# Top-32 attention with a hardswish MLP on one core: later batches' keys and queries transposed by DMA, and duos 2 to 19 at the wider spacing

## The chip, the core and the metric

The kernel runs on one core of a Trainium2 chip. A core has TensorE (PE, with PEld for its weight loads), VectorE (DVE), ScalarE (ACT), GpSimd (POOL) and SyncE (SP, which here issues all DMAs). Each takes its own instructions strictly in order, and they wait for each other through semaphores. The metric is the device time of one execution in microseconds (us).

## The reference

Attention over 8 batches of 8 heads, 576 positions, head size 64. Of each row of scores only the 32 largest survive; the result goes through a two-layer MLP with hardswish.

```python
scores = scale * np.matmul(q, k.transpose(0, 1, 3, 2))
kth = np.partition(scores, -32, axis=-1)[..., -32:-32 + 1]
scores = np.where(scores >= kth, scores, -1e9)
scores = scores - np.max(scores, axis=-1, keepdims=True)
attn = np.exp(scores); attn = attn / (np.sum(attn, axis=-1, keepdims=True) + 1e-09)
x = np.matmul(attn, v)            # then (B,H,S,D) -> (B*S, H*D) = (4608, 512)
h = x @ w_in                      # (4608, 2048)
out = (h * np.clip(h + 3.0, 0.0, 6.0) / 6.0) @ w_out
```

q, k and v are float32. The two weights arrive as float64 and are turned into float32 on the chip.

## The kernel before

Two heads make a **pair** (64 + 64 rows of TensorE), four pairs a batch. A pair's keys and queries are loaded as they lie (`Pair.load`, one tile `landed` of 128 x 1152 floats), and `Pair.transpose` (L170 to L182) turns them with nine 128 x 128 TensorE transposes into the one PSUM buffer `big`, from which ACT copies them out into `kq` and `kr`. The same `big` takes the scores.

Two pairs and 128 query positions make a **duo**: two rows of 576 scores in each partition for each of its two pairs. There are 80 duos, counted here from 0, ten in a batch. The 576 positions are four times 128 and a rest of 64, so in each of the batches 0 to 6 the duos 2 and 7 of the batch (2, 7, 12, 17, ... 67) are **rest duos** with half the rows; in the last batch these are 72 and 73. The steps of a duo m are

- `scores`: TensorE into `big`, ACT copies to `sc` (L232, L235; L218, L219 for a rest). It is called in slot 1 of duo m-1.
- `top`: DVE, four rounds of MAX8 and three of MATCH_REPLACE8 for each pair (L249, L253). This is what a duo's eight **slots** are: slots 0 to 3 are the rounds of its first pair, 4 to 7 those of the second.
- `shift` (POOL, L262, L265), `exp` (ACT: two Prelu L272, two Exp L277, the sum's epsilon L282), `inverse` (DVE reciprocal, L286), `weights` (POOL: scale L296, then split of each float into two 16-bit halves into tile `e16`, L305), `flip` (SP: DMA transpose of `e16` into `t16`, L311), `join` (halves put together again into `eT`, by ACT for the first pair and by POOL for the second, L317), `values` (TensorE, L337, copied out by ACT, L344). A 0 or 1 behind a step's name is the pair.

When these steps are called is written out in three tables, in slots from the duo's own slot 0: `early` for duos 0 and 1, `soon` for 2 to 19 and the last two, `usual` for 20 to 77. Each engine gets its instructions in the order of the calls:

```python
usual = dict(shift0=3, exp0=4, inverse0=7, weights0=8, flip0=10, join0=13,
    shift1=7, exp1=8, inverse1=11, weights1=12, flip1=14, join1=17, values=20)
soon = dict(shift0=3, exp0=3, inverse0=5, weights0=5, flip0=7, join0=10,
    shift1=7, exp1=7, inverse1=9, weights1=9, flip1=11, join1=14, values=16)
```

Between them `piece` emits the MLP in small **pieces** (four or eight matmuls of the first layer, L361, or two of the second, L383), 3 to 9 to a duo by how many are left; ACT copies a first-layer result out twice (L369, L371) and POOL gates it (L375, L376). `values` of some duos first empties the block before the last (a loop of `piece()`), so a few places get many pieces at once. What is left at the end is done after the last duo. In the first four and a half duos the weights are converted as well (`convert`, L102 to L122, on all of SP, ACT, POOL and DVE).

The tiles `landed`, `kq`, `e16`, `t16`, `eT` and the weights' `st` share one pool of 13 buffers (tag `kq`). A new tile waits until the buffer's last reader is done. For batch b+1 the four pairs are loaded in slot 0 of duos 4 to 7 of batch b and transposed in slot 5 of duos 5 to 8.

Of the kernel before, what the change touches and what calls it, by code (L numbers as in the profile page):

```python
# [10 lines left out]
F32 = mybir.dt.float32  # L11
U32 = mybir.dt.uint32
I32 = mybir.dt.int32
U16 = mybir.dt.uint16
# [15 lines left out]
def kernel(  # L30
# [9 lines left out]
    nc = tc.nc  # L40
    P = nc.NUM_PARTITIONS
    B, H, S, D = q.shape
    DM, FF = moe_w_in.shape
    J = S // P
    JP = J * P
    R = S - JP
# [6 lines left out]
    def pool(name, bufs, **kw):  # L53
        return ctx.enter_context(tc.tile_pool(name=name, bufs=bufs, **kw))

    consts = pool("consts", 1)
    kqpool = pool("kq", 13)
# [30 lines left out]
    def big():  # L88

        return ps_big.tile([P, 5 * 512], F32, tag="big", name="big")  # L90
# [47 lines left out]
    class Pair:  # L138
# [31 lines left out]
        def transpose(self):  # L170
            kq = kqpool.tile([P, JP + S], F32, tag="kq", name="kq")
            self.kT, self.qT = kq[:, 0:JP], kq[:, JP : JP + S]
            ps = big()
            for j in range(2 * J + 1):
                rows = self.landed[:, j, :, :].rearrange("p h d -> p (h d)")
                nc.tensor.transpose(ps[:, j * P : (j + 1) * P], rows, ident[:])
            c0 = 2 * JP
            nc.scalar.copy(kq[:, 0:c0], ps[:, 0:c0])
            nc.scalar.copy(kq[:, c0 : c0 + R], ps[:, c0 + R : c0 + 2 * R])
            for hh in range(2):  # L180
                d = slice(hh * D, (hh + 1) * D)
                nc.scalar.copy(self.kr[d, hh, :], ps[d, c0 : c0 + R])  # L182

    class Duo:

# [122 lines left out]
        def flip(self, u):  # L308
            t16 = self.t16[u] = kqpool.tile([P, 2 * (2 * J + 1), P], U16, tag="kq", name="t16")
            n = 2 * self.nb  # L310
            nc.sync.dma_start_transpose(t16[:, 0:n, :], self.e16[u][:, 0 : n * P])  # L311

        def join(self, u):

            eT = self.eT[u] = kqpool.tile([P, 2 * J + 1, P], F32, tag="kq", name="eT")
            copy = nc.gpsimd.tensor_copy if u else nc.scalar.copy
            copy(  # L317
                eT[:, 0 : self.nb, :]
                .rearrange("p c q -> p (c q)")
                .bitcast(U16)  # L320
                .rearrange("p (x h) -> p h x", h=2),
                self.t16[u][:, 0 : 2 * self.nb, :].rearrange("p (h c) q -> p h (c q)", h=2),
            )
# [79 lines left out]
    for b in range(B):  # L403
        halves = [pairs[b][0:2], pairs[b][2:4]]
# [8 lines left out]
    per_batch = 2 * J + 2  # L413
    ND = len(duos)
# [5 lines left out]
    def piece(count=1):  # L420
        nonlocal left
        for _ in range(count):
            while todo:
                try:
                    gates.append(next(todo[0]))
                    left -= 1
                    break
                except StopIteration:
                    todo.pop(0)
            else:  # L430
                gates.append(None)
            if len(gates) > 2:
                gate = gates.pop(0)
                if gate:
                    gate()
# [54 lines left out]
    def convert_step(depth=2):  # L490

        if len(converting) >= depth or not landing:
            for c in converting[:1]:
                next(c, None)
            del converting[:1]
        if landing:
            c = landing.pop(0)
            next(c)
            converting.append(c)
        land()  # L500

    def pair_at(m, first):

        b, at = divmod(m, per_batch)
        return pairs[b + 1][at - first] if b + 1 < B and 0 <= at - first < NHP else None
# [18 lines left out]
    usual = dict(  # L524
        shift0=3, exp0=4, inverse0=7, weights0=8, flip0=10, join0=13,
        shift1=7, exp1=8, inverse1=11, weights1=12, flip1=14, join1=17, values=20,
    )
    early = dict(
        shift0=3, exp0=3, inverse0=4, weights0=4, flip0=5, join0=7,
        shift1=7, exp1=7, inverse1=8, weights1=8, flip1=9, join1=10, values=11,  # L530
    )
    soon = dict(
        shift0=3, exp0=3, inverse0=5, weights0=5, flip0=7, join0=10,
        shift1=7, exp1=7, inverse1=9, weights1=9, flip1=11, join1=14, values=16,
    )
    queued = {}
    for m in range(ND):
        for part, at in (early if m < 2 else soon if m < 2 * per_batch or m >= ND - 2 else usual).items():
            queued.setdefault(8 * m + at, []).append((m, part))

    def parts(slot):
        for m, part in sorted(queued.get(slot, []), key=lambda x: x[1][:-1] != "shift"):
            if part == "values":
                values(m)
            else:
                getattr(duos[m], part[:-1])(int(part[-1]))

    for m in range(ND + 3):
        u = duos[m] if m < ND else None

        level = (left >= 8) + (left >= 16) + (left >= 48)
        count = ((3, 4, 4, 5) if u and u.rest else (6, 7, 8, 9))[level]
        for i in range(8):
            if u:
                u.top(i // 4, i % 4)
            convert_step()
            if m == 0 and i == 0:
                first[3].load()
            if m == 0 and i in (1, 2):
                first[i + 1].transpose()  # L560
            if i == (3 if m == 0 else 1) and m + 1 < ND:
                duos[m + 1].scores()
            parts(8 * m + i)
            if m == 0 and i in (1, 4):
                for p in duos[i // 4].pairs:
                    p.load_values()
            if i == 0:
                p = pair_at(m, 4)
                if p:
                    p.load()  # L570
            if i == 3 and u and u.pairs[0].b and 1 <= m % per_batch <= 2:
                for p in duos[m - 1].pairs:
                    p.load_values()
            if i == 5:
                p = pair_at(m, 5)
                if p:
                    p.transpose()
            piece((i + 1) * count // 8 - i * count // 8)
    while todo:
        piece()  # L580
# [34 lines left out]
```

## Time and profile before

| what | us |
| --- | --- |
| median of 3 runs | 1680.22 (1679.17 to 1680.78) |
| the profiled execution | 1679.66 |
| its span (first to last instruction) | 1677.9 |
| busy PE / DVE / ACT / POOL in the span | 1481.3 / 1469.5 / 1089.3 / 1144.2 |

The profile is of one execution. Its span is cut into stretches at the starts of duos: DVE's first MAX8 comes at 13.6 us, duo 3 starts at 116.9, duo 20 at 478.6, duo 72 at 1434.8; DVE's last MAX8 ends at 1579.8, and from there to 1677.9 the rest of the MLP runs. An undisturbed full duo takes DVE 19.4 us, an undisturbed rest duo about 11. A row's idle time in brackets is that of the engine just before the instruction, with what ended it. TensorE's records of a float32 matmul come in two, so its counts are twice the program's.

### The profile page before, as it was taken

Reading aid. Unit: us, or ns where it says so; the run is one execution under the profiler, and the core shown is the slowest. Engines: PE = TensorE matmul, PEld = TensorE weight load, DVE = VectorE, ACT = ScalarE, POOL = GpSimd, SP = SyncE. Lnnn points to the kernel's source line nnn. Section 1 sums busy time; section 2 is a strip of 40 time slices with the busy share of each in tenths; the row PEclk is TensorE's granted clock in tenths of the full one; section 3 lists DMA queues with packets and bytes.
Section 4 is the critical chain, followed back from the end, with each engine's and each line's share of the span. In section 5 each row is a group of like instructions: output and inputs, shape, how many; then the busy total and the mean of one; then the engine's idle time right before and its main releaser. Section 6 shows DMA issues by size and latency. Waiting matters only on the chain.

```text
span 1677.9 us, 25630 instructions
## 1 busy us (share of the span) xinstructions
PE 1481.3 (88%) x8736; PEld 985.9 (59%) x8736; DVE 1469.5 (88%) x3105; ACT 1089.3 (65%) x1863; POOL 1144.2 (68%) x1266
## 2 busy tenths in 40 slices
PE   5245688756899999899999999898999999899999
PEld 2142456534646757575766666565676675656775
DVE  5899979899799989999999979999999979999600
ACT  5556656656657868686767857677767766766621
POOL 4887566655657868685857857786867866776741
PEclk9567789977899999999999999999999999999999
DMA  8462433434235363445344432545345423433410
GB/s 235 132 185 52 92 62 63 100 73 85 56 62 106 76 120 54 94 87 109 60 96 96 86 82 54 117 81 112 62 94 100 97 57 74 96 64 64 70 21 13
DMA packets 450307, 144.29 MB, mean 86 GB/s; under 512 B 433280, under 2 KB 441472, under 8 KB 450176
## 3 DMA queue, kind: packets, MB, share of 16 engines
q1 hardware_dynamic: 450176, 142.65, 40.5%
q8 instruction: 69, 1.13, 0.3%
q14 instruction: 62, 0.51, 0.1%
HBM read 45.09 MB, written 9.44 MB: 32 GB/s over the span
## 4 chain that ended last, share of the span: by engine, by line
PE 45%; DVE 31%; POOL 10%; ACT 6%; issue 5%; DMA 2%; SPq 1%; POOLq 0%; ACTq 0%
PE acc L383 17%; DVE m L249 16%; PE h L361 15%; DVE wk L253 13%; PE pv L337 6%; PE big L226 4%; POOL eT L317 3%; POOL e L305 3%; POOL sc L296 2%; ACT eT L317 2%; ACT sc L277 1%; PE big L229 1%; POOL g L376 1%; DVE y L118 1%; DMA t<-e 1%
## 5 line engine op out<-in xcount | busy, mean ns | idle before, releaser
L249 DVE MAX8 m<-wk 128x8 f32<-128x576 f32 x864 | 614.8, 749 | 2.9
L383 PE MATMUL acc<-w_out,g 128*128 128x512 f32 x1152 | 515.8, 598 | 7.0 <-POOL g L376 7.0
L361 PE MATMUL h<-xT,w_in 128*128 128x256 f32 (+1 forms) x2560 | 470.7, 342 | 2.0 <-ACT hs L371 2.0
L361 PEld LDWEIGHTS h<-xT,w_in 128*128 128x128 f32 x2560 | 407.6, 193 | 50.0 <-issue 9.1
L253 DVE MATCH_REPLACE8 wk<-m,wk 128x576 f32<-128x576 f32 x576 | 424.4, 744 | 0.0
L383 PEld LDWEIGHTS acc<-w_out,g 128*128 128x128 f32 x1152 | 213.3, 191 | 246.0 <-issue 235.8
L305 POOL COPY e<-sc 128x2304 uint16<-128x2304 uint16 (+1 forms) x192 | 323.8, 1696 | 10.1
L337 PE MATMUL pv<-eT,vm 128*64 128x128 f32 (+1 forms) x2560 | 177.3, 286 | 159.3 <-POOL eT L317 122.5
L296 POOL TENSOR_SCALAR sc<-sc,den 128x576 f32<-128x576 f32 x288 | 213.3, 750 | 138.8 <-DVE den L286 137.8
L337 PEld LDWEIGHTS pv<-eT,vm 128*64 128x64 f32 x2560 | 143.8, 148 | 206.1 <-POOL eT L317 129.2
L277 ACT ACTIVATE sc<-sc,shift 128x576 f32<-128x576 f32 x288 | 220.1, 767 | 65.4 <-POOL shift L265 62.8
L272 ACT ACTIVATE sc<-sc,m 128x576 f32<-128x576 f32 x288 | 209.7, 774 | 59.5 <-DVE m L249 59.2
L317 POOL COPY eT<-t 128x2304 uint16<-128x2304 uint16 (+1 forms) x80 | 208.3, 2604 | 10.4 <-DMA t<-e 10.3
L317 ACT COPY eT<-t 128x2304 uint16<-128x2304 uint16 (+1 forms) x80 | 209.3, 2616 | 4.5 <-DMA t<-e 4.5
L253 DVE MATCH_REPLACE8 wk<-m,sc 128x576 f32<-128x576 f32 x288 | 212.1, 744 | 0.0
L249 DVE MAX8 m<-sc 128x8 f32<-128x576 f32 x288 | 203.3, 744 | 1.0 <-ACT sc L235 1.0
L376 POOL TENSOR_TENSOR g<-g,hs 128x512 f32<-128x512 f32 x144 | 183.7, 1276 | 12.2 <-POOL g L375 0.2
L262 POOL TENSOR_TENSOR shift<-m 128x2 f32<-128x2 f32 (+1 forms) x160 | 32.7, 204 | 195.5 <-DVE den L286 186.8
L232 ACT COPY sc<-big 128x2048 f32<-128x2048 f32 (+1 forms) x65 | 119.5, 1838 | 59.8 <-PE big L229 59.3
L375 POOL TENSOR_SCALAR g<-g 128x512 f32<-128x512 f32 x144 | 88.5, 615 | 98.7 <-ACT g L369 88.8
L226 PE MATMUL big<-kq 64*128 64x512 f32 x512 | 143.8, 684 | 8.5 <-ACT kr L182 8.4
L344 ACT COPY xT<-pv 128x256 f32<-128x256 f32 x64 | 23.8, 372 | 185.8 <-PE pv L337 185.8
(47 smaller groups left out, 1193.6 us busy)
## 6 DMA issues: line engine op xcount, KB each, us to landing
landed<-in_k_dram SPq DMA_DIRECT2D x64, 128.0 KB, 2.8
landed<-in_q_dram SPq DMA_DIRECT2D x64, 128.0 KB, 2.9
st<-in_moe_w_in_dram SPq DMA_DIRECT2D x16, 512.0 KB, 5.3
vm<-in_v_dram SPq DMA_DIRECT2D x64, 128.0 KB, 2.3
st<-in_moe_w_out_dram SPq DMA_DIRECT2D x16, 512.0 KB, 4.6
out_dram<-o SPq DMA_DIRECT2D x32, 256.0 KB, 2.4
t<-e SPq DMA_TRANSPOSE x160, 4.6
landed<-in_k_dram SPq DMA_DIRECT2D x32, 32.0 KB, 2.5
```

The costliest lines, as they stand in the source:

```text
L226: nc.tensor.matmul(banks[:, 2 * i + hh, :], pr.qT[d, qs], pr.kT[d, :])
L249: nc.vector.max(self.m[u][:, t, 8 * r : 8 * r + 8], self.cur[t])
L253: nc.vector.match_replace(wk, self.m[u][:, t, 8 * r : 8 * r + 8], self.cur[t], LOWEST)
L272: nc.scalar.activation(row, row, AF.Prelu, bias=m[:, t, TOP_K - 1 : TOP_K], scale=-1.0, alpha=FLAT)
L277: nc.scalar.activation(row, row, AF.Exp, bias=self.less[u][:, t : t + 1], scale=-scale / FLAT, accum_out=self.den[:, u, t : t + 1],)
L296: nc.gpsimd.tensor_scalar(row, row, self.den[:, u, t : t + 1], 1.0, ALU.mult, ALU.mult)
L305: nc.gpsimd.tensor_copy(halves[:, :, to : to + c1 - c0], words)
L317: copy(eT[:, 0 : self.nb, :] .rearrange("p c q -> p (c q)") .bitcast(U16) .rearrange("p (x h) -> p h x", h=2), self.t16[u][:, 0 : 2 * self ...
L337: nc.tensor.matmul(pv[hh * D : (hh + 1) * D, u * w : (u + 1) * w], pr.vm[:, hh, c, :] if c < J else pr.vr[:, hh, :], rhs, start=(c == 0), ...
L361: nc.tensor.matmul(h[:, (f - f0) * nt : (f - f0 + 1) * nt], w_in[:, i, f * P : (f + 1) * P], xT[:, i, 0:nt], start=(i == 0), stop=(i == NH ...
L376: nc.gpsimd.tensor_tensor(g[:], g[:], hs[:], ALU.mult)
L383: nc.tensor.matmul(acc[:], gs[f // nf][:, c0 : c0 + P], w_out[:, f, :], start=(f == 0), stop=(f == NFC - 1),)
```

## The change

Three things change. The pairs of batches 1 to 7 are no longer transposed by TensorE: POOL splits `landed` into 16-bit halves (`split`), SP issues a DMA transpose (`flip`), and ACT puts the halves together in `kq` and `kr` (`join`, four copies). The load comes a duo earlier (slot 0 of duos 3 to 6 of a batch), split and flip stand in slots 2 and 5 of duos 4 to 7, the join in slot 1 of duos 5 to 8. And the table `soon` now holds for the last two duos alone, so duos 2 to 19 go by `usual`; in `early`, the flips, joins and values of duos 0 and 1 come one or two slots later. Batch 0 is transposed as before.

```diff
+        def split(self):
+            self.e16 = kqpool.tile([P, 2 * (2 * J + 1) * P], U16, tag="kq", name="e16")
+            nc.gpsimd.tensor_copy(
+                self.e16[:].rearrange("p (h x) -> p h x", h=2),
+                self.landed[:]
+                .rearrange("p j h d -> p (j h d)")
+                .bitcast(U16)
+                .rearrange("p (x h) -> p h x", h=2),
+            )
+
+        def flip(self):
+            self.t16 = kqpool.tile([P, 2 * (2 * J + 1), P], U16, tag="kq", name="t16")
+            nc.sync.dma_start_transpose(self.t16[:], self.e16[:])
+
+        def join(self):
+            kq = kqpool.tile([P, JP + S], F32, tag="kq", name="kq")
+            self.kT, self.qT = kq[:, 0:JP], kq[:, JP : JP + S]
+            halves = self.t16[:].rearrange("p (h c) q -> p h (c q)", h=2)
+
+            def copy(dst, src):
+                nc.scalar.copy(dst.bitcast(U16).rearrange("p (x h) -> p h x", h=2), src)
+
+            c0 = 2 * JP
+            copy(kq[:, 0:c0], halves[:, :, 0:c0])
+            copy(kq[:, c0 : c0 + R], halves[:, :, c0 + R : c0 + 2 * R])
+            for hh in range(2):
+                d = slice(hh * D, (hh + 1) * D)
+                copy(self.kr[d, hh, :], halves[d, :, c0 : c0 + R])
...
     early = dict(
-        shift0=3, exp0=3, inverse0=4, weights0=4, flip0=5, join0=7,
-        shift1=7, exp1=7, inverse1=8, weights1=8, flip1=9, join1=10, values=11,
+        shift0=3, exp0=3, inverse0=4, weights0=4, flip0=6, join0=8,
+        shift1=7, exp1=7, inverse1=8, weights1=8, flip1=10, join1=12, values=13,
     )
...
-        for part, at in (early if m < 2 else soon if m < 2 * per_batch or m >= ND - 2 else usual).items():
+        for part, at in (early if m < 2 else soon if m >= ND - 2 else usual).items():
...
             if i == 0:
-                p = pair_at(m, 4)
+                p = pair_at(m, 3)
                 if p:
                     p.load()
...
-            if i == 5:
-                p = pair_at(m, 5)
+            for at, first_at, part in ((2, 4, "split"), (5, 4, "flip"), (1, 5, "join")):
+                p = pair_at(m, first_at) if i == at else None
                 if p:
-                    p.transpose()
+                    getattr(p, part)()
```

DVE in rest duo 12, from the reciprocal of duo 11's second pair to that of duo 12's first pair; before:

```order
L286 RECIPROCAL den<-den 128x2
L249 MAX m<-wk 128x8
L253 MATCH_REPLACE wk<-m,wk 128x576
L249 MAX m<-wk 128x8
L249 MAX m<-sc 128x8
L253 MATCH_REPLACE wk<-m,sc 128x576
L249 MAX m<-wk 128x8
L253 MATCH_REPLACE wk<-m,wk 128x576
L286 RECIPROCAL den<-den 128x1
```

and now (the lines behind the new methods are 30 higher):

```order
L316 RECIPROCAL den<-den 128x2
L279 MAX m<-sc 128x8
L283 MATCH_REPLACE wk<-m,sc 128x576
L279 MAX m<-wk 128x8
L283 MATCH_REPLACE wk<-m,wk 128x576
L279 MAX m<-wk 128x8
L283 MATCH_REPLACE wk<-m,wk 128x576
L279 MAX m<-wk 128x8
L316 RECIPROCAL den<-den 128x1
```

The first reciprocal stood behind the second round of duo 12 and stands behind the fourth; the second stood behind the sixth and stands behind the eighth. (One row before the second piece is the fourth round's MAX.)

ACT in rest duo 37, from the copy of duo 38's scores; before:

```order
L232 COPY sc<-big 128x4x512
L235 COPY sc<-big 128x2x128
L369 ACTIVATE g<-h,three 128x512
L371 COPY hs<-h 128x512
L344 COPY xT<-pv 128x2x128
L272 ACTIVATE sc<-sc,m 128x576
L277 ACTIVATE sc,den<-sc,shift 128x576
L282 ACTIVATE den<-den 128x1
L317 COPY eT<-t_5686 128x2x1152
L178 COPY kq<-big 128x1024
```

and now:

```order
L262 COPY sc<-big 128x4x512
L265 COPY sc<-big 128x2x128
L205 COPY kq<-t_5542 128x2x1024
L205 COPY kq<-t_5542 128x2x64
L205 COPY kr_112<-t_5542 64x2x64 x2
L399 ACTIVATE g<-h,three 128x512
L401 COPY hs<-h 128x512
L374 COPY xT<-pv 128x2x128
L302 ACTIVATE sc<-sc,m 128x576
L307 ACTIVATE sc,den<-sc,shift 128x576
L312 ACTIVATE den<-den 128x1
L347 COPY eT<-t_5611 128x2x1152
```

The join of a pair of batch 4 (three rows, four copies, from a transposed tile `t`) now stands between the scores' copy and duo 37's exp; before, the copies from `big` stood behind that exp.

TensorE in duos 46 and 47, up to the scores of duo 48 (`kr_110`); before:

```order
L383 MATMUL acc<-w_out,g 128x512 x6
L337 MATMUL pv<-eT,vm_104 64x128 x8
L337 MATMUL pv<-eT,vr_108 64x128 x2
L337 MATMUL pv<-eT,vm_105 64x128 x8
L337 MATMUL pv<-eT,vr_109 64x128 x2
L383 MATMUL acc<-w_out,g 128x512 x2
L176 MATMUL big<-ident,landed 128x128 x9
L383 MATMUL acc<-w_out,g 128x512 x6
L226 MATMUL big<-kq 128x512 x4
L229 MATMUL big<-kr_110,kq 128x128
```

and now:

```order
L413 MATMUL acc<-w_out,g 128x512 x6
L367 MATMUL pv<-eT,vm_104 64x128 x8
L367 MATMUL pv<-eT,vr_108 64x128 x2
L367 MATMUL pv<-eT,vm_105 64x128 x8
L367 MATMUL pv<-eT,vr_109 64x128 x2
L413 MATMUL acc<-w_out,g 128x512 x8
L256 MATMUL big<-kq 128x512 x4
L259 MATMUL big<-kr_110,kq 128x128
```

The nine transposes between the pieces are gone; the pieces of the MLP and the values (`pv`) stand as they did.

## Rows read from the trace of the kernel before

**Rows 1.** Page, part 1: busy time, share of the span, instructions of each engine.

```profile
PE 1481.3 (88%) x8736; PEld 985.9 (59%) x8736; DVE 1469.5 (88%) x3105; ACT 1089.3 (65%) x1863; POOL 1144.2 (68%) x1266
```

**Rows 2.** DVE's waits to 116.9, to 478.6, to 1434.8: us, times, longest.

```profile
DVE den L286 <- ACT den L282: 15.4, 4, 7.5
...
DVE den L286 <- ACT den L282: 44.1, 19, 5.5
...
DVE den L286 <- ACT den L282: 27.0, 8, 10.0
```

**Rows 3.** Windows, stretches: length, busy PE, PEld, DVE, ACT, POOL, clock, DMA share, GB/s.

```profile
116.90:478.60 361.70, 269.13 (x1689) 181.48 (x1689) 316.57 (x669) 221.78 (x379) 230.41 (x255) 0.84 0.37 75
478.60:1434.80 956.20, 933.60 (x5378) 611.97 (x5373) 925.12 (x1986) 679.36 (x1165) 689.92 (x764) 0.99 0.43 87
...
1579.80:1677.90 98.10, 94.11 (x572) 67.34 (x570) 0.17 (x1) 22.27 (x38) 31.54 (x31) 0.99 0.13 23
```

**Rows 4.** Timeline, rest duo 12: start, length, engine, instruction, idle time before it.

```profile
318.33 0.78 ACT L277 ACTIVATE sc<-sc,shift 128x576 f32<-128x576 f32 x1 [4.06 <-POOL shift L265]
...
320.23 0.17 DVE L286 RECIPROCAL den<-den 128x2 f32<-128x2 f32 x1 [3.60 <-ACT den L282]
...
325.30 2.82 ACT L317 COPY eT<-t 128x2304 uint16<-128x2304 uint16 x1
...
329.97 0.16 DVE L286 RECIPROCAL den<-den 128x1 f32<-128x1 f32 x1 [4.10 <-ACT den L282]
```

**Rows 5.** Timeline, duo 0 into duo 1: ACT's join.

```profile
50.68 2.78 ACT L317 COPY eT<-t 128x2304 uint16<-128x2304 uint16 x1 [2.34 <-DMA t<-e]
```

**Rows 6.** Groups by line and form: count, busy us, mean ns, idle before.

```profile
L317 ACT COPY eT<-t 128x2304 uint16<-128x2304 uint16 x64 | 178.5, 2789 | 4.5 <-DMA t<-e 4.5
...
L317 ACT COPY eT<-t 128x1536 uint16<-128x1536 uint16 x16 | 30.8, 1925 | 0.0
...
L305 POOL COPY e<-sc 128x2304 uint16<-128x2304 uint16 x128 | 271.7, 2123 | 8.1
...
L178 ACT COPY kq<-big 128x1024 f32<-128x1024 f32 x32 | 32.2, 1006 | 7.2 <-PE big L176 7.2
...
L182 ACT COPY kr<-big 64x64 f32<-64x64 f32 x64 | 13.3, 208 | 0.4
```

**Rows 7.** Timeline, rest duo 37.

```profile
799.03 0.37 ACT L344 COPY xT<-pv 128x256 f32<-128x256 f32 x1 [2.63 <-PE pv L337]
...
801.07 0.20 ACT L282 ACTIVATE den<-den 128x1 f32<-128x1 f32 x1
...
802.01 0.14 DVE L286 RECIPROCAL den<-den 128x1 f32<-128x1 f32 x1
```

**Rows 8.** Timeline, duos 46 and 47.

```profile
954.08 2.78 POOL L317 COPY eT<-t 128x2304 uint16<-128x2304 uint16 x1
957.40 1.09 PE L337 MATMUL pv<-eT,vm 128*64 128x128 f32 x16
...
961.55 1.15 PE L176 MATMUL big<-ident,landed 128*128 128x128 f32 x9
...
970.25 13.90 PE L383 MATMUL acc<-w_out,g 128*128 128x512 f32 x32
...
988.25 0.37 ACT L344 COPY xT<-pv 128x256 f32<-128x256 f32 x1 [3.47 <-PE pv L337]
...
990.53 0.16 DVE L286 RECIPROCAL den<-den 128x1 f32<-128x1 f32 x1 [9.99 <-ACT den L282]
```

**Rows 9.** Windows, as rows 3: duos 34, 37 and 45.

```profile
732.50:751.90 19.40, 19.40 (x110) 12.90 (x109) 19.40 (x44) 16.37 (x28) 17.31 (x19) 1.00 0.36 72
...
790.70:802.10 11.40, 9.01 (x68) 7.73 (x67) 10.99 (x25) 8.62 (x17) 10.88 (x12) 0.86 0.49 100
...
930.40:949.80 19.40, 19.04 (x118) 14.38 (x116) 19.40 (x44) 15.88 (x29) 18.18 (x19) 1.00 0.47 84
```

**Rows 10.** DMA issues: queue, operation, count, us from issue to landing.

```profile
t<-e SPq DMA_TRANSPOSE x160, 4.6
```

## The prediction

> **What bounds the kernel now.** I read the page's busy shares first, then DVE's waits by stretch, then the windows, and last the timeline at the places where DVE waits. PE and DVE are both busy for 88% of the span [rows 1], so the average does not say which of them sets the time; the stretches do. From duo 20 to duo 72 DVE works 925.1 of 956.2 us and PE 933.6 [rows 3]: both are full. From duo 3 to duo 20 DVE works 316.6 of 361.7 and PE 269.1 [rows 3], and what DVE stands still for there is one thing: 19 waits, 44.1 us, of its reciprocal for ACT's `den` [rows 2]. To 116.9 the same wait costs 15.4 us in 4 times, from 478.6 to 1434.8 it costs 27.0 in 8 [rows 2]. So the kernel runs at DVE's pace from its first MAX8 at 13.6 us to its last at 1579.8, plus those waits, and then 98.1 us of MLP without DVE follow [rows 3]. The changed program emits as many pieces of the MLP as before up to each duo from 27 on, so this tail holds the same work. The question is how many of the 44.1 + 15.4 + 27.0 us go, and what comes in their place.
>
> **Duos 2 to 19 at the usual spacing.** Rest duo 12 shows both kinds of the wait. The reciprocal of duo 11's second pair waits 3.60 us because Exp had to wait 4.06 us for POOL's `shift`, which stood behind POOL's split, join and gates; the one of duo 12's first pair waits 4.10 us because ACT's 2.82 us join stood ahead of the exp [rows 4]. From Exp's start to the reciprocal 1.9 us pass (318.33 to 320.23), and the two Prelus ahead need 1.4 more. `soon` gives this chain two slots, 3 us in a rest duo and about 5 in a full one; `usual` gives three, 4 and 7 us, and calls the join of the duo before behind the exp. The nearest evidence for what is left is the stretch that goes by `usual` already: of its 27.0 us in 8 waits [rows 2] two take 10 us each, in duos 47 [rows 8] and 67, which PE holds up (below), and the six others share 7, more than half of it in duo 27, held up in the same way; all eight are in rest duos, the full ones have none, and in duos 34 and 45 DVE is busy for 19.40 of 19.40 us [rows 9]. So I expect about 0.4 at each of the rest duos 7, 12 and 17, say 1 us, of the 44.1. Duos 7 and 17 get a join of keys on top, and the buffers and POOL's splits can hold ACT or POOL a little; for both together I take 4 us (bounds 1 and 20, worked out below). **Term: 44.1 - 1 - 4 = 39 us less.**
>
> Values come four slots later in these duos, so the MLP starts later: up to the scores of duo 20 the program now emits 88 pieces where it emitted 90. PE has idle time there (92 us of 361.7, at 0.84 of its clock [rows 3]) and makes up the two pieces by duo 27. With the stretch 39 us shorter, PE has 323 us for its 269 less eight groups of transposes; that still fits at the clock granted now.
>
> **Duos 0 and 1.** The largest of the four waits, 7.5 us [rows 2], belongs to duo 0's first pair, whose slots don't change. In two of the others ACT's join, which itself waited 2.34 us for the DMA [rows 5], stood ahead of the exp in slot 7 and now stands a slot behind it. That frees ACT earlier, but the chain from DVE's last MAX8 through Prelu and Exp (3.3 us by the rows above) stays in one slot, so most of the wait stays: **0.8 us less**, between 0 and 4.
>
> **The transposes of 28 pairs.** *Removed:* nine transposes on PE, 1.15 us a pair [rows 8], and ACT's copies of 1.0 us and three of 0.2 [rows 6]: 32 us of PE, 46 of ACT in all. *Added:* a POOL split, 128 x 2304 halves, 2.12 us as the same copy of `e16` [rows 6], 59 us; a DMA transpose, 4.6 us to landing [rows 10]; and ACT's join. Its price is not in the trace; from the two sizes of the other join (2304 halves 2.79 us, 1536 halves 1.93 [rows 6]) a half costs 1.13 ns and a copy 0.2 us, so 2048 halves and three times 128 cost 2.5 + 3 x 0.34 = 3.5 us, 1.9 more than the copies it replaces.
>
> Where do these lie? The join now stands in slot 1 ahead of an exp that stands in slot 4. In a full duo three slots (over 7 us) of slack cover it. In rest duo 37 ACT waits 2.63 us for `pv` before the exp, and its `den` is done 0.7 us ahead of the reciprocal (801.27 against 802.01) [rows 7]. The join takes the 2.63 first, then 0.7 of what is left: 3.5 - 2.63 - 0.7 leaves 0.2, taken as 0.5. Duos 7, 17, 37 and 57 are like this, the first two in the 4 us above: **1 us more** for the others, 0 to 5.
>
> Rest duo 47 is the other kind, and 27 and 67 resemble it. DVE waits 9.99 us there because PE does 13.90 us of pieces in one go behind the scores of duo 48, then values, and ACT's exp stands behind the copy of those values [rows 8]. The join hides in ACT's wait. Ahead of these pieces PE now leaves out one group of transposes, 1.15 us, in duo 46, and one in duo 45. But the second gain ends at once: `pv` of duo 44 starts at 957.40 and needs POOL's `eT`, done at 956.86 [rows 8], and POOL gets 2.12 us more in a duo where it is busy for 18.18 of 19.40 [rows 9], so `eT` may come 2 us later. Together between 1.5 us less and 2 us more for each of the three; I take **0**.
>
> Here a rule of the Trainium skill speaks against the change. The Trainium skill, page VectorE: DVE Perf Modes, sections "The three transpose paths" and "Rules for kernel authors", gives 390 ns for a 128 x 128 bf16 transpose on TensorE and 1309 ns by the DMA crossbar, and advises TensorE where PSUM will do. The rows agree that the new way is the longer one for a pair. By the rule the sum would get a loss where mine has none, because in my sum nothing waits for the landing; the rival below prices it.
>
> **Sum.** 1679.7 - 39 - 0.8 + 1 = 1640.9 for the profiled execution, which lay 0.6 us below the median; I say **1641**.
>
> **Rivals.**
> *The waits come back in another shape.* Two tiles more per pair turn over in the 13 buffers. In the new program, ACT's join in duo 6 gets a buffer that PE's values of duo 4 read last, called three slots later, and so in duo 15; in duo 16 POOL's join does. ACT and POOL then stand until PE is there, with exp or `shift` queued behind. For it: POOL's `shift` already cost 4.06 us so. Against it: PE is not full there [rows 3], and the spacing leaves 3 us of slack. If half of the 39 us return, 1660.
> *PE's relief counts fully.* Waits at 27, 47 and 67 shrink by two groups and the gaps around them (about 3 us each) and duos 0 and 1 give 4: 1641 - 9 - 3 = 1629.
> *The landing shows.* A rest duo has three DMA transposes in five slots (7 us), and each takes 4.6 [rows 10]. If two joins in each of 7 rest duos wait a full landing, less the 2.63 us that ACT has free [rows 7], 14 x 2 = 28 us come back: 1669. The lead of four slots and more speaks against it. This is what the skill's rule on the three transpose paths amounts to here.
> *POOL becomes the bound, and the change is slower.* In duos 34 and 45 POOL is busy for 17.31 and 18.18 us of 19.40 [rows 9], and 2.12 more makes 19.4 and 20.3. If that delay runs on through `shift`, `eT` and the gates to DVE for all four splits of a batch, 28 x 2.12 = 59 us come: 1700. It decides only if POOL has less than 2.1 us free in nearly every such duo; duo 37, busy for 10.88 of 11.40 [rows 9], is of that kind, but duos next to it have many us free, so that the excess should be 1 us a batch.
>
> **How the numbers follow.** Forecast (1633 to 1649) 0.58; waits come back by a quarter or more, 1649 to 1668, 0.17; full relief, 1620 to 1633, 0.11; landing or other loss up to no change 0.08; slower by POOL 0.06. What a measurement can tell from no change is about 0.2%, 3.4 us. Faster 0.91, same 0.03, slower 0.06. The range 1627 to 1661 leaves some 0.2 out: the two last cases, and the ends of the second and third.
>
> **What would show it.** Right: DVE's wait for `den` between duos 3 and 20 falls from 44.1 to about 5 us, duo 20 starts near 439, duos 47 and 67 still wait 8 to 12 us, the tail stays near 98. Wrong: waits of ACT's join for PE or for the DMA, or of `shift` behind POOL's split, with DVE idle behind them; or a full duo between 20 and 71 that takes over 19.5 us.

## The result and the profile after

| | before | after |
| --- | --- | --- |
| median, us (4 runs each) | 1680.25 | 1637.51 (1637.13 to 1638.8) |
| after / before | | 0.9748 (0.9731 to 0.9765) |
| span of the profiled execution | 1677.9 | 1637.0 |
| duo 3 / 20 / 72 starts | 116.9 / 478.6 / 1434.8 | 113.8 / 433.5 / 1393.3 |
| last MAX8 ends, rest of the MLP | 1579.8, 98.1 | 1538.6, 98.4 |

The change makes the kernel 2.5% faster: 1637.5 us, where 1641 was forecast with a range of 1627 to 1661. The time went where the forecast looked for it, but its terms hold to different degrees, and one of the two halves of the change, the transposes by DMA, costs time. Page of after, part 1 and the row of part 6 on the transposes, against [rows 1, 10]:

```profile
PE 1452.6 (89%) x8484; PEld 960.5 (59%) x8484; DVE 1470.0 (90%) x3105; ACT 1141.7 (70%) x1863; POOL 1201.0 (73%) x1294
...
t<-e SPq DMA_TRANSPOSE x188, 4.6
```

TensorE lost 28.7 us of work, ACT got 52.4 and POOL 56.8; DVE does the same work as before. The median over all DMA transposes, from issue to landing, is still 4.6 us. DVE's waits for `den` of after, in the four stretches of [rows 2] (to 113.8, to 433.5, to 1393.3) and in the whole span (total, times, longest):

```profile
DVE den L316 <- ACT den L312: 10.9, 4, 7.6
...
DVE den L316 <- ACT den L312: 3.0, 3, 1.3
...
DVE den L316 <- ACT den L312: 30.7, 7, 11.1
...
DVE den L316 <- ACT den L312: 54.9, 20, 11.1
```

Stretch by stretch the waits went from 15.4 to 10.9, from 44.1 to 3.0 and from 27.0 to 30.7 us. Windows of after for duos 3 to 19, 20 to 71 and the tail, columns as in [rows 3]:

```profile
113.80:433.50 319.70, 255.63 (x1641) 175.75 (x1640) 315.50 (x671) 236.82 (x380) 242.44 (x259) 0.87 0.48 96
433.50:1393.30 959.80, 924.08 (x5215) 596.60 (x5214) 925.03 (x1987) 717.36 (x1166) 735.98 (x787) 0.98 0.50 99
1538.60:1637.00 98.40, 94.17 (x572) 67.34 (x570) 0.21 (x2) 22.33 (x38) 31.68 (x31) 0.99 0.10 23
```

The first stretch is 42.0 us shorter (361.7 to 319.7), the second 3.6 longer although TensorE works 9.5 us less in it. The waits grow in duos 27 (4.3 to 8.6 us) and 67 (9.9 to 11.1) and shrink in 22 (1.5 to nothing) and 47 (10.0 to 9.5). Duos 27, 47 and 67 are the place where the forecast took nothing, and the experiments turn on it.

### The profile page after: what moved, and what is told of

Its sections match the earlier page's. It is cut to its first block, busy times and chain, and to the rows that moved or that the text cites. A ratio compares the mean times of both kernels' runs of the same rounds, so it can differ in the third digit from the quotient of the medians.

```text
span 1637.0 us, 25149 instructions
## 1 busy us (share of the span) xinstructions
PE 1452.6 (89%) x8484; PEld 960.5 (59%) x8484; DVE 1470.0 (90%) x3105; ACT 1141.7 (70%) x1863; POOL 1201.0 (73%) x1294
## 4 chain that ended last, share of the span: by engine, by line
DVE 58%; PE 25%; POOL 10%; ACT 3%; issue 2%; SPq 1%; DMA 0%; POOLq 0%; ACTq 0%
DVE m L279 30%; DVE wk L283 25%; PE acc L413 10%; PE h L391 9%; PE pv L367 3%; POOL eT L347 3%; PE big L256 2%; POOL sc L326 2%; POOL e L335 2%; DVE y L118 1%; POOL g L406 1%; ACT sc L307 1%; DVE a L117 1%; POOL g L405 1%; PE big L259 1%
## 5 line engine op out<-in xcount | busy, mean ns | idle before, releaser
L391 PE MATMUL h<-xT,w_in 128*128 128x256 f32 (+1 forms) x2560 | 479.2, 346 | 0.0
L391 PEld LDWEIGHTS h<-xT,w_in 128*128 128x128 f32 x2560 | 416.0, 196 | 52.6 <-issue 12.8
L399 ACT ACTIVATE g<-h,three 128x512 f32<-128x512 f32 x144 | 98.5, 684 | 61.4 <-PE h L391 59.1
L256 PE MATMUL big<-kq 64*128 64x512 f32 x512 | 133.0, 638 | 5.7 <-ACT kr L182 5.7
L262 ACT COPY sc<-big 128x2048 f32<-128x2048 f32 (+1 forms) x65 | 119.3, 1835 | 24.8 <-PE big L259 24.7
```

What stands on the lines that cost most here:

```text
L256: nc.tensor.matmul(banks[:, 2 * i + hh, :], pr.qT[d, qs], pr.kT[d, :])
L391: nc.tensor.matmul(h[:, (f - f0) * nt : (f - f0 + 1) * nt], w_in[:, i, f * P : (f + 1) * P], xT[:, i, 0:nt], start=(i == 0), stop=(i == NH ...
```

## The experiments

Two theories stood first. S: the spacing is the whole gain, by the order in ACT's and POOL's queues, and the transposes cost or give little. T: the transposes free TensorE and ACT's copies, and much of the gain is theirs. The runs, each with its ratio to the kernel before as measured beside it, DVE's waits for `den` in all (us) and those of rest duos 27, 47 and 67:

| kernel | us | by before | waits | 27, 47, 67 |
| --- | --- | --- | --- | --- |
| before | 1680.3 | 1 | 96.5 | 4.3, 10.0, 9.9 |
| after | 1637.5 | 0.9748 | 54.9 | 8.6, 9.5, 11.1 |
| spacing only | 1631.4 | 0.9714 (0.970 to 0.9729) | 47.5 | 5.9, 9.7, 10.0 |
| DMA transposes only | 1713.2 | 1.0201 (1.0184 to 1.0218) | 129.9 | 5.0, 11.1, 11.1 |
| after, old `early` | 1639.7 | 0.9763 (0.9748 to 0.9777) | 57.2 | 8.6, 9.5, 11.1 |
| before, `soon`'s join behind exp | 1660.2 | 0.9876 (0.9862 to 0.9891) | 77.5 | 4.3, 9.8, 10.0 |
| after, keys' join in slot 5 | 1635.8 | 0.9729 (0.9713 to 0.9745) | 52.3 | 6.7, 10.9, 9.2 |
| after, split in slot 6 | 1637.4 | 0.974 (0.9725 to 0.9754) | 53.2 | 8.4, 11.5, 11.5 |
| after, split on ACT | 1632.9 | 0.972 (0.9704 to 0.9735) | 48.7 | 4.0, 7.5, 7.5 |
| spacing only, POOL copy added | 1638.3 | 0.9755 (0.9736 to 0.9773) | 54.4 | 7.5, 11.3, 11.3 |
| after, exp first | 1620.0 | 0.9645 (0.9631 to 0.9659) | 35.0 | gone |
| after, split on ACT, exp first | 1622.8 | 0.9661 (0.9646 to 0.9676) | 39.4 | 0, 0.3, 0 |
| spacing only, exp first | 1615.2 | 0.9609 (0.9595 to 0.9623) | 31.5 | gone |

### The two halves apart

Spacing only is the kernel before with the new tables (`early`, and `usual` from duo 2 on); DMA transposes only is the kernel after with the old tables:

```diff
-    for part, at in (early if m < 2 else soon if m < 2 * per_batch or m >= ND - 2 else usual).items():
+    for part, at in (early if m < 2 else soon if m >= ND - 2 else usual).items():
```

> The kernel before with the new tables alone (duos 2 to 19 by usual, early's flips, joins and values later); keys and queries are still transposed by TensorE. Theory S (the spacing is the whole gain): DVE's wait for den between duos 3 and 20 falls from 44.1 us to 1 to 4, that of duos 0 to 2 from 15.4 to about 11, the three heavy rest duos keep 24 us or get the 1.7 us of one piece more in duo 27; 1635 to 1642 us. Rival T (taking the transposes off TensorE is what made room): at least 10 us of the 44 stay, 1650 or more.

> The changed kernel with the old tables (soon for duos 2 to 19, old early): only the DMA transposes are new. Theory S: nothing gained; ACT's 3.5 us join in slot 1 stands ahead of an exp with two slots only, so a few us more at duos 5 to 7 and 15 to 17: 1680 to 1692 us. Rival T: 1665 or less.

Measured 1631.4 and 1713.2 us. S holds, and more sharply than it was put, for both times lie outside its ranges: the spacing alone gives 48 us (0.0286 of the time before), more than the whole change and more than the 38 to 45 that S expected. The transposes cost 6.1 us on top of the spacing and 34 without it, where S had at most 12. Waits for `den` of spacing only, between duos 3 and 20 and then to duo 72:

```profile
DVE den L286 <- ACT den L282: 0.3, 1, 0.3
...
DVE den L286 <- ACT den L282: 26.8, 6, 10.0
```

Of the 44.1 us 0.3 are left. Why the transposes cost so much at the old spacing is seen in ACT's queue of DMA transposes only, in the full duo 5 (timeline, ACT and then DVE's reciprocal):

```profile
181.09 2.68 ACT L205 COPY kq<-t 128x2048 uint16<-128x2048 uint16 x2
183.63 0.67 ACT L205 COPY kr<-t 64x128 uint16<-64x128 uint16 x2
184.32 0.60 ACT L423 ACTIVATE o<-acc 128x512 f32<-128x512 f32 x1
184.94 2.75 ACT L347 COPY eT<-t 128x2304 uint16<-128x2304 uint16 x1
187.56 1.43 ACT L302 ACTIVATE sc<-sc,m 128x576 f32<-128x576 f32 x2
...
190.78 0.17 DVE L316 RECIPROCAL den<-den 128x2 f32<-128x2 f32 x1 [4.41 <-ACT den L312]
```

The keys' join (3.2 us, 181.09 to 184.32) and the join of the duo before (2.75) stand ahead of Prelu and Exp, in a chain that the old table gives two slots. The new table calls the join of the duo before behind the exp and gives the chain a third slot; the keys' join is then alone ahead of the exp, and in full duos it is covered. So the two halves are not additive: the spacing saves 28 of the 34 us.

### Is it the order in the queues?

The kernel before, with one number of `soon` changed, so that in duos 2 to 19 and the last two the join of the duo before comes behind the exp and not ahead of it:

```diff
-        shift0=3, exp0=3, inverse0=5, weights0=5, flip0=7, join0=10,
+        shift0=3, exp0=3, inverse0=5, weights0=5, flip0=7, join0=13,
```

> The kernel before with one number changed: in soon, join0 goes from 10 to 13, so that ACT's join stands behind the exp of the next duo; reciprocals, weights and values stay. By the trace of before, 26.7 of the 44.1 us of waits between duos 3 and 20 have that join directly ahead of the exp, 17.4 have POOL's work ahead of the shift. Theory (order in the queue): about 20 of the 26.7 go, the 17.4 stay, 1656 to 1663 us. Rival (two slots from exp to reciprocal are too few whatever is ahead): more than half of the 26.7 stay, 1667 or more.

Measured 1660.2 us, within the first theory's range. One call in another place takes 20 us; between duos 3 and 20 24.7 us in 11 waits stay, some 17 of them behind POOL's `shift`:

```profile
DVE den L286 <- ACT den L282: 24.7, 11, 4.1
```

So some two fifths of the spacing's gain are ACT's order. The rest comes with the other entries of the new tables: the third slot for the chain, and weights, joins and values that are called later. No run takes these apart.

### The parts at duos 0 and 1

The kernel after with the old `early` table (`flip0=5, join0=7 ... values=11`).

> The changed kernel with the old table early for duos 0 and 1. If the 4.6 us that the waits of duos 0 to 2 lost (15.4 to 10.8) come from early's later joins, they come back: 1640 to 1643 us, three waits of 1.8, 3.5 and about 2.5 us in duos 1 and 2. If they come from elsewhere (usual for duo 2), 1637 to 1638.

Measured 1639.7, just under the range of the first theory. In duo 1 the waits of 1.83 and 3.52 us return, where after has 0.6 each, and in duo 2 one of 2.5 where after has 2.0; with duo 0, which waits 0.6 less, 4.0 us of wait come back, of which 2.2 show in the time.

```profile
56.70 0.17 DVE L316 RECIPROCAL den<-den 128x2 f32<-128x2 f32 x1 [1.83 <-ACT den L312]
76.34 0.17 DVE L316 RECIPROCAL den<-den 128x2 f32<-128x2 f32 x1 [3.52 <-ACT den L312]
```

### What in the transposes costs: ACT's join?

The keys' join four slots later than in the change, away from the exp, and in a second kernel the split as well:

```diff
-            for at, first_at, part in ((2, 4, "split"), (5, 4, "flip"), (1, 5, "join")):
+            for at, first_at, part in ((2, 4, "split"), (5, 4, "flip"), (5, 5, "join")):
...
+            for at, first_at, part in ((6, 4, "split"), (1, 5, "flip"), (5, 5, "join")):
```

> The changed kernel with the keys' join (ACT) moved from slot 1 to slot 5, behind the exp, everything else as it is. If the join ahead of the exp makes the waits of 1.3 us in duos 7 and 17 and part of those in the heavy rest duos: 7 and 17 fall to about 0.4, duo 67 (11.1 us) by 1 or more, 1633 to 1636 us. If POOL's split and TensorE's pieces make them, only the 1.8 us of duos 7 and 17 go, or nothing: 1635.5 to 1638.

> The changed kernel with POOL's split in slot 6 instead of slot 2, the flip in slot 1 and the join in slot 5 of the next duo, so that POOL no longer has the split ahead of the shift and the second pair's join. If the split is what makes TensorE's values late (2.3 us of waiting for eT ahead of duo 27), the waits of duos 27, 47 and 67 fall from 8.6, 9.5 and 11.1 us to about 6, 9 and 9.5: 1630 to 1634 us, near the kernel that has the spacing alone (1631.4). If not, as with the join in slot 5 alone.

Measured 1635.8 and 1637.4: 1.7 us and nothing. The waits of 1.3 us at duos 7 and 17 stay in the first and go in the second (0.3 and none), so they are the split's. But with the split in slot 6 TensorE still stands for 2.2 us for POOL's `eT` ahead of duos 27, 47 and 67, and the waits there are together 2.0 us longer. Moving the split by a few slots moves its price.

The first kernel looks like a gain for the theory of the join: 2.0 and 1.9 us less at 27 and 67, but 1.4 more at 47. TensorE's granted clock explains these changes better. In after it falls for a while in duos 26 and 66, in this kernel in 46 alone, and in the kernel with the split in slot 6 in all three; each time the next rest duo waits longer. Windows of duos 26 and 46 of the first kernel (columns as in [rows 3], the clock third from the right), and the same 16 records of `acc` in each:

```profile
541.60:561.00 19.40, 17.22 (x86) 8.31 (x82) 19.40 (x45) 16.22 (x24) 15.47 (x16) 1.00 0.62 121
905.10:924.50 19.40, 17.63 (x76) 8.33 (x74) 19.40 (x44) 15.78 (x25) 16.48 (x17) 0.91 0.57 113
...
552.66 7.13 PE L413 MATMUL acc<-w_out,g 128*128 128x512 f32 x16
...
915.23 8.83 PE L413 MATMUL acc<-w_out,g 128*128 128x512 f32 x16
```

So one fall less, 1.5 to 1.7 us of TensorE, is enough for the 1.7 us, and no gain from the place of ACT's join is shown. Only the profiled execution of each kernel tells where the clock fell.

### What costs: POOL's split

Two kernels, one that takes the split off POOL and one that puts it into the kernel without DMA transposes. In the first ACT makes the split (slot 5; flip and join behind it); in the second a POOL copy of the split's size is added to the spacing-only kernel (slot 2 of duos 5 to 8 of a batch, where the change splits in 4 to 7), its result unused:

```diff
-            nc.gpsimd.tensor_copy(
+            nc.scalar.copy(
-            for at, first_at, part in ((2, 4, "split"), (5, 4, "flip"), (1, 5, "join")):
+            for at, first_at, part in ((5, 4, "split"), (7, 4, "flip"), (5, 5, "join")):
...
+            if i == 2:
+                p = pair_at(m, 5)
+                if p:
+                    p.split()
```

> The changed kernel with the split into halves done by ScalarE (slot 5, on the same four duos of a batch) in place of GpSimd, and the flip and the keys' join two slots later, so that they still follow it. Theory P (GpSimd's split makes eT late ahead of duos 27, 47 and 67, TensorE then stands for some 2 us, and VectorE pays for that): these standing times of TensorE go below 0.5 us, the granted clock of TensorE is 1.00 all through duos 26, 46 and 66, the waits for den at 27, 47 and 67 are at most 6, 10 and 10 us, and the time is 1628 to 1632 us. Rival J (GpSimd is not it; the transposes cost through ScalarE's join or through the piece of the MLP more in one go): TensorE's standing times may go, but the waits at 27, 47 and 67 stay 8, 10 and 11 us or grow with ScalarE's 2 us more a duo, and the time is 1635 us or more.

> The kernel with the new spacing alone (TensorE's transposes, no DMA transposes) and one GpSimd copy added to the second slot of four duos of a batch, of the size and place of the change's split into halves; its result is used by nothing. Theory P (the split by itself makes eT late): TensorE stands for 1.5 to 2.5 us ahead of duos 27, 47 or 67 as in the changed kernel, waits for den are 7 to 9 us at 27, 10 to 11.5 at 47 and 67, about 1 at 7 and 17, and the time is 1635 to 1640 us, against 1631.4 without the copy. Rival: GpSimd has the room, eT isn't late, and the time is 1630 to 1633 us.

The second is plain: 1638.3 us against 1631.4 without the copy. 28 copies of 2.1 us on POOL, which nobody waits for, cost 6.9 us, about as much as the whole of the transposes does (6.1). Waits of this kernel between duos 3 and 20 and then to duo 72, beside 3.0 and 30.7 of after:

```profile
DVE den L296 <- ACT den L292: 2.6, 2, 1.3
...
DVE den L296 <- ACT den L292: 31.1, 6, 11.3
```

And the way it goes, in rest duo 7 of the same kernel: POOL, ACT, DVE.

```profile
211.20 2.10 POOL L186 COPY e<-landed 128x2304 uint16<-128x2304 uint16 x1
213.27 0.19 POOL L272 TENSOR_TENSOR shift<-m 128x1 f32<-128x1 f32 x1
...
213.81 0.78 ACT L287 ACTIVATE sc<-sc,shift 128x576 f32<-128x576 f32 x1 [2.14 <-POOL shift L275]
...
214.94 0.16 DVE L296 RECIPROCAL den<-den 128x1 f32<-128x1 f32 x1 [1.29 <-ACT den L292]
```

The split stands ahead of `shift`, Exp waits for `shift`, the reciprocal for Exp. In after the same place reads 211.09 for the split, 1.06 us of Exp's wait and 1.30 of the reciprocal's. Ahead of duos 27, 47 and 67 the delay takes a longer way. In after it is POOL's `eT` that TensorE's values need. The split of duo 26 stands behind that `eT`; late is the queue that the split of duo 25 pushed back, in which POOL has no idle time up to it: `eT` is done 10.0 us into duo 26, against 7.1 in spacing only (timelines of POOL, then of TensorE, duo 25 into duo 28):

```profile
532.45 2.11 POOL L187 COPY e<-landed 128x2304 uint16<-128x2304 uint16 x1
...
549.00 2.77 POOL L347 COPY eT<-t 128x2304 uint16<-128x2304 uint16 x1
...
551.82 1.09 PE L367 MATMUL pv<-eT,vm 128*64 128x128 f32 x16 [2.31 <-POOL eT L347]
...
553.06 8.83 PE L413 MATMUL acc<-w_out,g 128*128 128x512 f32 x16
561.82 1.99 PE L256 MATMUL big<-kq 64*128 64x512 f32 x8
...
564.29 10.47 PE L413 MATMUL acc<-w_out,g 128*128 128x512 f32 x24
574.59 1.89 PE L391 MATMUL h<-xT,w_in 128*128 128x256 f32 x8
576.41 1.09 PE L367 MATMUL pv<-eT,vm 128*64 128x128 f32 x16
```

TensorE stands for 2.31 us, everything behind it is as much later and more, since its clock falls as well (last section), and DVE pays at the next rest duo, where ACT's exp stands behind the copy of those last values. In the kernel with the added copy TensorE waits in the same duos too (1.82, 1.46 and 1.72 us in 26, 46 and 66, against some 0.5 in spacing only), but for the copies of the keys: ACT waits for `shift`, and these stand behind ACT's exp. What was expected, that it would be `eT` again, was wrong in this. ACT's Exp of duo 25, then TensorE:

```profile
535.70 0.78 ACT L287 ACTIVATE sc<-sc,shift 128x576 f32<-128x576 f32 x1 [1.18 <-POOL shift L275]
...
542.64 1.08 PE L224 MATMUL big<-kq 64*64 64x512 f32 x4 [1.82 <-ACT kr L182]
```

So the copy shows that 2.1 us on POOL are dear at these places. At 7 and 17 it costs what the split costs in after (2.6 us of wait either way). At 27, 47 and 67 the way is another (4.4 us of wait, against 3.6 in after, part of it the clock's), so that the two sums are nearly equal is partly luck.

The split on ACT is a miss by 1 us for the first theory (1632.9, 1628 to 1632 expected) and better than its rival allowed (1635). What that theory said of TensorE came: it stands for `eT` for 0.43 us in duo 26 and the granted clock is 1.00 all through duos 26, 46 and 66. The waits at 27, 47 and 67 are 4.0, 7.5, 7.5, which is 10.3 us less than in after and 6.7 less than without DMA transposes. So POOL's split is what makes them long in after, and TensorE's relief is real. It is eaten elsewhere: seven full duos behind the rest duos (8, 18, ... 68) now wait some 1 us each, 6.8 in all, where ACT makes the join, the split and the keys' join in one row ahead of the exp:

```profile
576.32 2.76 ACT L347 COPY eT<-t 128x2304 uint16<-128x2304 uint16 x1
578.95 2.10 ACT L187 COPY e<-landed 128x2304 uint16<-128x2304 uint16 x1
580.95 2.67 ACT L205 COPY kq<-t 128x2048 uint16<-128x2048 uint16 x2
583.49 0.67 ACT L205 COPY kr<-t 64x128 uint16<-64x128 uint16 x2
...
587.26 0.16 DVE L316 RECIPROCAL den<-den 128x1 f32<-128x1 f32 x1 [1.01 <-ACT den L312]
```

### What is left, and a faster version

Some 19 to 31 us stand at 27, 47 and 67 in every kernel so far, because in a slot the values' matmuls, and ACT's copy of them, were issued ahead of the exp. In the next kernels the exp goes first:

```diff
-    for m, part in sorted(queued.get(slot, []), key=lambda x: x[1][:-1] != "shift"):
+    for m, part in sorted(queued.get(slot, []), key=lambda x: (x[1][:-1] != "shift", x[1][:-1] != "exp")):
```

> The changed kernel with exp called ahead of the other steps of a slot, so that ACT's exp of a rest duo no longer stands behind the copy of values, which TensorE's pieces hold up. Theory: the waits of 8.6, 9.5, 11.1 and 2.7 us in duos 27, 47, 67 and 76 go below 1 us each and 25 to 32 us of time with them, since TensorE catches up in the duos behind: 1606 to 1614 us. Rival: TensorE is behind for good there, the waits come back in the next duos or as a longer tail: 1625 to 1638.

> The kernel before with the new tables and with exp called first in its slot; TensorE transposes stay, no DMA transposes. If the gains add up: 1631.4 less what exp first gave the changed kernel (17.5 us), 1611 to 1617 us. If TensorE, which keeps its 28 groups of transposes, is then the bound: 1618 to 1626.

> The kernel with the split on ScalarE and, in each slot, the exp issued ahead of the values' matmuls. If the two edits add (the exp's order took 17.5 us off the changed kernel, 16.2 off the kernel with the new spacing alone), the time is the split-on-ScalarE kernel's less 15 to 18 us: 1610 to 1616 us by theory P, level with the spacing and exp order without DMA transposes (1615.2). By rival J it is 1617 us or more. The waits for den at duos 27, 47 and 67 are gone either way, and some 30 us of waits in 11 to 16 duos stay at the duos behind them.

Measured 1620.0, 1615.2 and 1622.8. The edit takes 17.5 us from after, 16.2 from spacing only, 10.1 from the split on ACT. For the first this lies between what the two theories expected; the second came as expected if the gains add; for the last the two edits don't add, and the rival's bound (1617 or more) holds. The waits at 27, 47, 67 and 76 go in all three (0.3 us stay at 47 in the third), but others come a duo later: 2.4, 5.0 and 5.0 us at 28, 48 and 68 in the first, 1.3, 5.2 and 5.4 in the second, 3.3, 6.3 and 6.7 in the third, and for the 2.6 at 76 some 3.7 at 77 and 78. In duo 48 ACT still stands for TensorE's values first, and then the exp stands behind a row of joins and copies (second kernel; ACT, then DVE):

```profile
933.92 0.37 ACT L344 COPY xT<-pv 128x256 f32<-128x256 f32 x1 [3.47 <-PE pv L337]
934.19 2.78 ACT L317 COPY eT<-t 128x2304 uint16<-128x2304 uint16 x1
936.83 1.01 ACT L178 COPY kq<-big 128x1024 f32<-128x1024 f32 x1
...
938.30 0.69 ACT L369 ACTIVATE g<-h,three 128x512 f32<-128x512 f32 x1
938.89 0.58 ACT L371 COPY hs<-h 128x512 f32<-128x512 f32 x1
939.35 0.79 ACT L272 ACTIVATE sc<-sc,m 128x576 f32<-128x576 f32 x1
...
941.37 0.16 DVE L286 RECIPROCAL den<-den 128x1 f32<-128x1 f32 x1 [5.21 <-ACT den L282]
```

With the split on ACT these waits are the longest; that ACT's longer queue makes them so is argued, and no run shows it alone.

The second kernel, the new spacing with the exp first and TensorE's transposes kept, is the fastest: 0.9609 (0.9595 to 0.9623) of before.

## Why the prediction was right, point by point

**What bounds.** Right. DVE's busy time is what it was (1470.0 us), and the span shrank by 40.9 us while its waits for `den` shrank by 41.6.

**Duos 2 to 19: 39 us less.** Right. Measured 41.1 (44.1 to 3.0), with 1.3, 0.4 and 1.3 at duos 7, 12 and 17, and duo 20 at 433.5 where 439 was expected. The mechanism was the right one: the spacing alone leaves 0.3, and one join's place alone makes 20 us of it. Of the 4 us set aside for the keys' join and POOL's splits 2.6 came, and from the split, not from the join. That the third slot is needed, as the forecast argued, no run shows by itself.

**Duos 0 and 1: 0.8 us less, up to 4.** Mis-sized. Duo 3 starts 3.1 us earlier, the waits fell by 4.5 us (15.4 to 10.9), and the old table costs 2.2 us of the time. The step that failed is "most of the wait stays": once the join no longer stood ahead of the exp, the wait of 3.5 us in duo 1 shrank to 0.6, though the chain has one slot as before.

**Two pieces made up by duo 27, at nothing.** Wrong. In duo 27 TensorE does 24 records of `acc` in one go, 10.47 us, where it did 20 before; that is one piece more, 1.7 us. Spacing only shows this by itself: 5.9 us of wait at duo 27 against 4.3. Before, then spacing only:

```profile
608.52 8.75 PE L383 MATMUL acc<-w_out,g 128*128 128x512 f32 x20
...
558.89 10.47 PE L383 MATMUL acc<-w_out,g 128*128 128x512 f32 x24
```

**The transposes: 1 us more.** The direction was right and the size was not: 6.1 us, or 3.5 beside the 2.6 in the term above. The durations were close: split 2.1 us (2.12 taken), keys' join 3.2 (3.5 taken), landing 4.6 and hidden. The step that failed is the 0 us for duos 27, 47 and 67, in which TensorE's two groups (2.3 us) were set against a later `eT`. It gave up to 2 us more for each as a bound; after against spacing only has 2.7, -0.2 and 1.1. The weighing itself was nearly right: TensorE stands for `eT` for 2.31, 1.91 and 1.93 us, and at 47 the two cancel. What it left out is the clock, which falls behind that standing in duos 26 and 66 and takes 1.5 to 1.7 us more of TensorE each time; where the kernel with the later keys' join has no fall, 27 and 67 wait 6.7 and 9.2. The 1 us taken for 37 and 57 was 0.3 at 37 and nothing at 57 (0.3 before as after).

**The rivals.** The waits did not come back in another shape: 3.0 us in 3 waits are left between duos 3 and 20. The landing did not show; ACT stands still for 0.2 us in all ahead of the 28 keys' joins, so nothing pointed to 1669. The Trainium skill, page VectorE: DVE Perf Modes, section "The three transpose paths", has the crossbar as the slower path, and section "Rules for kernel authors" advises TensorE. That choice is right here (1631.4 against 1637.5), but the price that the runs show lies in the split that this kernel makes of its float32 data ahead of the crossbar, not in the landing. POOL as the bound was the rival with the right engine and the wrong scale: 59 us if every split ran through, 6.9 in the run that has the split alone, since DVE feels it in a few rest duos only. Full relief of TensorE did not come, though the split on ACT shows 6.7 us of it at 27, 47 and 67.

**The total** came out close because errors of two signs met, which is partly luck. By the starts of duos the profiled execution gained 3.1 us to duo 3 and 42.0 from there to duo 20, 5.3 more than was taken, and lost 3.6 us to duo 72 and 0.6 behind it, 3.2 more than was taken: 2.1 us below the forecast. The median of the four runs lies another 1.3 lower (1637.5; they go from 1637.1 to 1638.8).

## What to carry to other kernels

Look first at what stands ahead of the late chain's next link in each in-order queue. Moving one join behind the exp took 20 us, and issuing the exp ahead of the values 16, without removing any work. When work goes to another engine to relieve a full one, price it by the queue in which it lands, at the tightest place: 2.1 us on POOL in four duos of a batch cost 6.9 us, though POOL was busy for 70% of the span and TensorE for 90% (page of spacing only). Two edits of which one lengthens a chain and the other gives it room have to be run apart: here one was worth 48 us, and the other cost 6.1 with it and 34 without.

## What the runs showed of the hardware

TensorE's clock fell in the midst of a full stretch. Windows of after round TensorE's wait of 2.31 us for `eT` in duo 26 (columns as in [rows 3], the granted clock third from the right):

```profile
541.80:553.10 11.30, 8.99 (x67) 4.79 (x63) 11.30 (x27) 8.23 (x14) 10.98 (x11) 1.00 0.52 107
553.30:556.50 3.20, 3.20 (x5) 1.14 (x5) 3.20 (x9) 3.17 (x7) 3.04 (x6) 0.50 0.89 165
556.70:561.20 4.50, 4.50 (x11) 1.97 (x11) 4.50 (x10) 3.76 (x4) 1.17 (x1) 1.00 0.79 162
```

After the wait the clock is at the lower of its two levels (0.50 in these rows, 1.2 GHz), from about 553 to 556.5 us, although TensorE is busy all through. It fell in the same way in duo 66, after a wait of 1.93 us, and not in duo 46, after one of 1.91. The same 16 records of `acc` took 7.13 us in duo 46 and 8.60 in duo 66:

```profile
917.67 7.13 PE L413 MATMUL acc<-w_out,g 128*128 128x512 f32 x16
...
1284.17 8.60 PE L413 MATMUL acc<-w_out,g 128*128 128x512 f32 x16
```

So a wait of 2 us can cost 1.5 us more behind it, about the difference between the waits at 67 and 47 (11.1 and 9.5). How long TensorE waited does not tell whether the clock falls: with the keys' join in slot 5 it fell after 1.77 us (duo 46) and not after 2.18 (duo 26). The Trainium skill, page TensorE: Matmul & The Clock Gate, section "Part 1: The HAM clock gate", says that a monitor of TensorE's recent activity sets the clock to full or half; the trace agrees with the two levels, and no run here shows why duo 46 was spared. In after the two falls take some 3.2 us of TensorE (8.83 and 8.60 in place of 7.13, twice), about half of the 6.1 us that the transposes cost there. They are not needed for a loss: the kernel with the added POOL copy has none in duos 26, 46 and 66 and takes as long as after. With the split on ACT the clock does not fall in these duos, and the only wait of TensorE over 0.4 us in them is the one of 0.43.
